# Regrouping the last weight loads and splitting the final accumulator of a decode block by output quadrants

## The chip, the cores and the metric

One core of one Trainium2 chip runs the whole program. The metric is the device time of one execution in microseconds (us). TensorE does the matmuls, VectorE (DVE) and ScalarE (ACT) the elementwise work, GpSimd (POOL) a few fills, and SyncE (SP) issues nearly all DMAs.

## The reference, cut to what matters

```python
h  = x + attention(layernorm(x), k_cache, v_cache, wq) @ wo      # x: 4 tokens x 448
y  = layernorm(layernorm(h))
g  = gelu(y @ w1 + b1)                                          # 4 x 1792
h2 = h + g @ w2 + b2                                            # 4 x 448
```

The case is a decode step: four tokens, one each, against a cache of 1024 positions in eight groups of heads. Nearly all of its bytes are the caches and the weights, read once. Only the last line, `h + g @ w2 + b2`, is touched here.

## The kernel before, in words

SP issues all loads in one fixed order: eleven packed streams with queries, keys, values and output weights, then the last values, the last output weights, `w1`, and `w2`. They go through a ring of three slots of SBUF, so a load is issued when its slot is free, long before its data are wanted. TensorE's order is written out by hand; the other engines follow by semaphores.

**The second product of the MLP.** `w2` has 1792 rows. They are held as 14 chunks (`w2t[c]`): chunks 0 to 11 and the chunks 12 and 13, each 128 rows by 448 columns. The 448 output columns are four groups of C = 112. Output group j is computed on partitions 32j to 32j+31, called quadrant j. So each chunk is four matmuls of 128x32 weights (the transposed activations `gT`) with 112 columns of `w2`, one for each quadrant (line 510). A result that is first set up with `h + b2` (line 489) stays in one PSUM tile `py` for all four quadrants, and all 14 chunks add to it.

**How w2 is loaded (lines 380 to 389).** SP issues five pieces in this order: chunks 0 to 7 (1792 KB), chunks 8 to 10 (672 KB), then `w2_low` as two DMAs of 28 KB, then chunks 11 and 12 (448 KB), last the columns of quadrants 0 to 2 of chunk 13 (168 KB). `w2_low` is quadrant 3 of chunk 13, folded: its 128 rows are laid on 64 partitions as two pieces side by side, in DRAM as eight blocks of four rows (with a row left out between blocks), and the other 64 partitions are filled with zeros by POOL (line 381). In that form it takes two matmuls (line 516) with weights from `gT_low`, which DVE fills (line 506).

**The order on TensorE (lines 508 to 516).** The loop goes over c = 0 to 13 and j = 0 to 3; the two `w2_low` matmuls come in chunks 9 and 10 behind j = 1. The waits for the loads stand in this order: chunk 0 waits for the first piece, chunk 8 for the second, the first `w2_low` matmul for both small pieces, chunk 11 for the fourth, chunk 13 for the last.

**The end (lines 517 to 520).** DVE copies `py` to `res` in SBUF. Two DMAs of 4 KB store its halves: ACT issues the one of quadrants 2 and 3, SP the one of quadrants 0 and 1. Both wait for the copy. The program ends when both have landed.

**ACT before that.** Its last work is the gelu (line 480), with an activation table loaded for it ahead of time.

Of the kernel before, what the change touches and what calls it, by code (L numbers as in the profile page):

```python
# [8 lines left out]
F32 = mybir.dt.float32  # L9
# [6 lines left out]
B, D = 4, 448  # L16
# [4 lines left out]
P = 128  # L21
H = P // 2
ND = 4
NKC = W // P
NFC = F // P
FQ = F // 4
Q = 32
GAP = Q // B
LIFT = Q - B
# [34 lines left out]
W1C = 3 * F + F // 2  # L64
C = D // 4
PAD = 3 * (P - C)
W2L = NFC * D - C
EPS = 1e-5
SCALE = DH ** -0.5

# [1 line left out]
def block_kernel(ctx: ExitStack, tc, first, streams, v7, wo67, w1, w2, w2_low, out):  # L72
    nc = tc.nc
    const = ctx.enter_context(tc.tile_pool(name="const", bufs=1))
    ring = ctx.enter_context(tc.tile_pool(name="ring", bufs=3))
    work = ctx.enter_context(tc.tile_pool(name="work", bufs=2))
    once = ctx.enter_context(tc.tile_pool(name="once", bufs=1))
    ps_s = ctx.enter_context(tc.tile_pool(name="ps_s", bufs=2, space=PSUM))
    ps_t = ctx.enter_context(tc.tile_pool(name="ps_t", bufs=1, space=PSUM))
    ps_o = ctx.enter_context(tc.tile_pool(name="ps_o", bufs=1, space=PSUM))  # L80
    ps_m = ctx.enter_context(tc.tile_pool(name="ps_m", bufs=2, space=PSUM))
    ps_w = ctx.enter_context(tc.tile_pool(name="ps_w", bufs=1, space=PSUM))
# [80 lines left out]
    pT = [const.tile([P, NKC // 2, B, Q], F32, name=f"pT{i}") for i in range(2)]  # L163
    oT = [const.tile([P, 4, Q], F32, name=f"oT{i}") for i in range(2)]
    gT = const.tile([P, NFC, LIFT + Q], F32, name="gT")
    gT_low = const.tile([P, 2, Q], F32, name="gT_low")
    idle = const.tile([P, 512], BF16, name="idle")
    nc.vector.memset(idle, 0.0)
    back = const.tile([P, 4, LIFT + Q], F32, name="back")
# [4 lines left out]
    def beside(t, j):  # L174
        return t[:, :Q] if j % 2 == 0 else t[:, LIFT:]
# [48 lines left out]
    def scores(g):  # L224
        s = [ps_s.tile([P, 512], F32, tag="s", name=f"s{g}_{h}") for h in range(2)]
        mx = work.tile([P, 2], F32, tag="mx", name=f"mx{g}")
        for h in range(2):
            for c in range(2):
                for b in range(B):
                    nc.tensor.matmul(  # L230
                        s[h][b * Q : (b + 1) * Q, :], qT[g % 2][:, c, b, :], load_k(g, h, c)[:, b, :],
                        start=(c == 0), stop=(c == 1),
                    )
            nc.vector.reduce_max(mx[:, h : h + 1], s[h], axis=AX.X)  # L234
        nm = work.tile([P, 1], F32, tag="nm", name=f"nm{g}")
        nc.vector.tensor_max(nm, mx[:, 0:1], mx[:, 1:2])
        nc.vector.tensor_scalar_mul(nm, nm, -SCALE)  # L237
        p = work.tile([P, 2 * 512], F32, tag="p", name=f"p{g}")
        sums = work.tile([P, 2], F32, tag="sums", name=f"sums{g}")
        for h in range(2):  # L240
            nc.scalar.activation(  # L241
                p[:, h * 512 : (h + 1) * 512], s[h], AF.Exp, bias=nm, scale=SCALE,
                accum_out=sums[:, h : h + 1],
            )
        rec = work.tile([P, 1], F32, tag="rec", name=f"rec{g}")
        nc.vector.tensor_add(rec, sums[:, 0:1], sums[:, 1:2])
        nc.vector.reciprocal(rec, rec)
        return p, rec
# [24 lines left out]
        return po  # L273


    acc = ps_w.tile([P, D], F32, name="acc")


    def columns(t, j):
# [4 lines left out]
    def heads(g, po, rec):  # L284
        o = work.tile([P, 2, DH], F32, tag="o", name=f"o{g}")
        nc.vector.tensor_scalar_mul(o[:, :, :P], po[:, :, :P], rec)  # L286
        nc.scalar.mul(o[:, :, P:], po[:, :, P:], rec)  # L287
        pt = ps_m.tile([P, 512], F32, tag="m", name=f"pot{g}")
        if g in (HKV - 3, HKV - 1):
            keep_warm(3 if g == HKV - 1 else 5, pt)  # L290
        for c in range(2):
            for i in range(2):
                at = (2 * i + c) * P - i * REP
                nc.tensor.transpose(pt[:, at : at + P], o[:, i, c * P : (c + 1) * P], ident)  # L294
        if g >= HKV - 2:
            keep_warm(1)
        dst = oT[g % 2].rearrange("p (r c) (b e) -> p r (c b) e", r=REP, b=B)[..., 0]
        src = pt.rearrange("p (i k q) -> p q k i", i=2, q=Q)[:, :REP]
        nc.vector.tensor_reduce(dst, src, axis=AX.X, op=ALU.add)
# [60 lines left out]
    for g in range(HKV):  # L360
        if g + 1 < HKV:
            p, rec_next = scores(g + 1)
            if g == HKV - 2:
                heads(g - 1, *late)
            if g + 2 < HKV:
                project_q(g + 2, wq_parts(part("q", g + 2)))
            transpose_p(g + 1, p)
            if g + 1 == HKV - 1:
                keep_warm(2, ps_m.tile([P, 512], F32, tag="m", name="wait"))
                tail.append(ps_t.tile([P, 2, 512], F32, tag="t", name="tail"))  # L370
                keep_warm(5)
        else:
            v7t = load_v7()
            tw = slot("w1")
            wo_last = [wo_rows(tw[:, i * WC : (i + 1) * WC]) for i in range(2)]
            nc.sync.dma_start(tw[:, : 2 * WC], wo67)
            tw1 = tw[:, 2 * WC : 2 * WC + W1C]
            for a, n in ((0, 2 * F), (2 * F, W1C - 2 * F)):
                nc.sync.dma_start(tw1[:, a : a + n], w1[:, a : a + n])
            tw2 = slot("w2")  # L380
            nc.gpsimd.memset(tw2[H:, W2L : W2L + 2 * C], 0.0)
            at = 0
            for n in (8 * D, 3 * D, 0, 2 * D, 3 * C):
                if n:
                    nc.sync.dma_start(tw2[:, at : at + n], w2[:, at : at + n])
                else:
                    for h in range(2):
                        nc.sync.dma_start(tw2[h * Q : (h + 1) * Q, W2L : W2L + 2 * C], w2_low[h, :, : Q // 8, :])
                at += n
        if g == HKV - 1:  # L390
            keep_warm(5)
        po = values(g, v7t if g == HKV - 1 else None)
        if g == HKV - 2:
            project_o(g - 1, wo_rows(part("o", g - 1)))
        if g == HKV - 3:
            late = po, rec
        else:
            heads(g, po, rec)
        if g < HKV - 3:
            project_o(g, wo_rows(part("o", g)))  # L400
        if g == HKV - 2:
            accs = once.tile([P, 4 * P], F32, tag="u", name="accs")[:, :D]
            nc.scalar.copy(accs, acc)
            hsum = ps_s.tile([P, 512], F32, tag="s", name="hsum")[:, :P]
            ph = hsum.rearrange("p (i c) -> p i c", i=2)
            pu = ps_s.tile([P, 512], F32, tag="s", name="pu")[:, :FQ]
            for j in range(4):
                nc.tensor.matmul(ph[j * Q : (j + 1) * Q], sel, columns(accs, j), start=True, stop=False)  # L408
        if g == HKV - 1:
            keep_warm(5)  # L410
            for i in range(2):
                project_o(HKV - 2 + i, wo_last[i])
        if g + 1 < HKV:
            rec = rec_next

    w1t = [tw1[:, a * F : (a + 1) * F] for a in range(3)] + [tw1[:, 3 * F :]]
    w2t = [tw2[:, c * D : (c + 1) * D] for c in range(NFC)]
# [17 lines left out]
    h = once.tile([P, P], F32, tag="h", name="h")  # L435
    hb = once.tile([P, PAD + P + C], F32, tag="hb", name="hb")
# [26 lines left out]
    for a in range(ND):  # L463
        for j in range(4):
            rows, w = w1_part(a, j)
# [14 lines left out]
        nc.scalar.activation(u[:, cols], u[:, cols], AF.Gelu_apprx_tanh)  # L480

    keep_warm(2)
    py = ps_o.tile([P, C], F32, tag="o", name="py")
    for i in range(2):
        for j in range(4):
            if i <= j:
                at = PAD + C * j - P * (j - 1 + i) if j else PAD
                lhs = back[:, j - 1 + i if j else 0, :]
                nc.tensor.matmul(
                    py[j * Q : (j + 1) * Q], beside(lhs, j), hb[:, at : at + C], start=(i == 0), stop=False,  # L490
                )
    keep_warm(2)
    res = once.tile([P, P], F32, tag="res", name="res")
    nc.gpsimd.memset(res, 0.0)
    put = ps_m.tile([P, 3 * P], F32, tag="m", name="put")
    for c in range(3):
        nc.tensor.transpose(put[:, c * P : (c + 1) * P], u[:, c * P : (c + 1) * P], ident)
# [5 lines left out]
    halves = put2.rearrange("p (s j i b e) -> p s i j b e", s=2, j=2, i=2, b=B)[..., 0]  # L503
    for side, i, rows in ((0, 0, slice(0, H)), (1, 1, slice(H, P))):
        nc.vector.tensor_copy(gT[rows, 12:NFC, LIFT:Q], halves[rows, side, i])
    nc.vector.tensor_copy(gT_low[:H, :, :B], halves[:H, 0, :, 1])
    nc.tensor.matmul(tail[0][:Q, 0, :Q], gT[:, 0, :Q], gT[:, 0, :Q], start=True, stop=True)
    for c in range(NFC):
        for j in range(4 if c < NFC - 1 else 3):
            nc.tensor.matmul(  # L510
                py[j * Q : (j + 1) * Q], beside(gT[:, c, :], j), w2t[c][:, j * C : (j + 1) * C],
                start=False, stop=(c == NFC - 1 or (c == NFC - 2 and j == 3)),
            )
            if j == 1 and 9 <= c < 11:
                w = tw2[:, W2L + (c - 9) * C : W2L + (c - 8) * C]
                nc.tensor.matmul(py[3 * Q :], gT_low[:, c - 9, :], w, start=False, stop=False)  # L516
    nc.vector.tensor_copy(res[:, :C], py)  # L517
    for i, queue in ((1, nc.scalar), (0, nc.sync)):
        at = i * H + LIFT
        queue.dma_start(out[2 * B * i : 2 * B * (i + 1)], res[at : at + 2 * B])  # L520


# [67 lines left out]
```

## Time and profile before

| | |
|---|---|
| median of 3 runs | 213.80 us (213.77 to 213.82) |
| the profiled execution's own time | 213.79 us |
| its span in the trace | 212.0 us |
| mean granted TensorE clock | 0.871 |
| DMA, mean over the span | 417 GB/s |

The profile is one execution. Times in its rows count from the start of the span; the execution's own time is 1.8 us longer than the span. PE is a matmul, PEld a weight load, SPq and ACTq are DMA issues of SP and ACT. In this trace each matmul of line 510 shows as two records of each kind.

### The profile page before, as it was taken

The numbers are of one execution on the slowest core, as the hardware profiler recorded it, in microseconds if no ns is written. First come the engines' busy times: TensorE is split into PE (matmuls) and PEld (weight loads), VectorE is DVE, ScalarE is ACT, GpSimd is POOL, SyncE is SP. The second block draws the span as 40 slices with busy tenths as digits, with TensorE's granted clock in tenths as the row PEclk, the third lists the DMA queues.
The fourth block names the chain that finished last, engine by engine and source line by source line (L and its number), as shares of the span: only waits on it lengthen the run. The fifth ranks groups of instructions, "written<-read, shape, count | busy, mean of one in ns | idle before, by whom it ended". The sixth has DMA issues, their size and how long they took to land.

```text
span 212.0 us, 2559 instructions
## 1 busy us (share of the span) xinstructions
PE 142.4 (67%) x1103; PEld 55.5 (26%) x1103; DVE 37.0 (17%) x153; ACT 24.5 (12%) x58; POOL 6.5 (3%) x22
## 2 busy tenths in 40 slices
PE   0469805861860885870794780586499998989994
PEld 0333301220110511220122120131124333335443
DVE  1521400320130110320123011031032032101330
ACT  2011300110001100210003000030002002100310
POOL 6200000000000000000000000000000000000110
PEclk9999975896697579996589698599589999999999
DMA  7999798999989999898999989899999899999991
GB/s 297 437 407 510 340 512 383 460 446 398 480 355 507 393 449 452 386 483 347 510 414 436 468 383 469 365 490 398 464 414 444 378 467 399 408 434 417 416 404 58
DMA packets 3146, 88.39 MB, mean 417 GB/s; under 512 B 368, under 2 KB 576, under 8 KB 960
## 3 DMA queue, kind: packets, MB, share of 16 engines
q1 hardware_dynamic: 3120, 88.24, 97.0%
q8 instruction: 8, 0.13, 0.2%
q14 instruction: 2, 0.02, 0.0%
q10 hardware_dynamic: 16, 0.00, 0.0%
HBM read 88.23 MB, written 0.01 MB: 416 GB/s over the span
## 4 chain that ended last, share of the span: by engine, by line
DMA 79%; PE 18%; ACT 1%; issue 0%; SPq 0%; DVE 0%; ACTq 0%
DMA stream<-stream 69%; DMA w<-w 10%; PE s L230 6%; PE po L269 6%; PE ppt L255 2%; PE py L510 2%; PE pq L207 1%; PE pqt L215 1%; ACT qs L209 1%; PE acc L304 0%; SPq L98 0%; SPq L100 0%; DVE res L517 0%; PE py L516 0%; ACTq L209 0%
## 5 line engine op out<-in xcount | busy, mean ns | idle before, releaser
L230 PE MATMUL s<-stream,qT 128*32 128x512 f32 x256 | 37.4, 730 | 17.1 <-DMA stream<-stream 17.1
L269 PE MATMUL po<-stream,pT 128*32 128x512 f32 x224 | 31.6, 702 | 17.5 <-DMA stream<-stream 17.5
L234 DVE TENSOR_REDUCE mx<-s 128x1 f32<-128x512 f32 x16 | 11.1, 691 | 57.3 <-PE s L230 57.3
L230 PEld LDWEIGHTS s<-stream,qT 128*32 128x32 f32 x256 | 9.7, 132 | 42.6 <-issue 30.6
L207 PE MATMUL pq<-stream,yT 128*32 128x512 f32 (+1 forms) x80 | 10.2, 603 | 9.7 <-DMA stream<-stream 6.6
L269 PEld LDWEIGHTS po<-stream,pT 128*32 128x32 f32 x224 | 6.9, 124 | 35.3 <-DMA stream<-stream 20.4
L286 DVE TENSOR_SCALAR o<-po,rec 128x256 f32<-128x256 f32 x8 | 3.9, 483 | 60.1 <-PE po L269 60.1
L209 ACT COPY qs<-pq 128x512 f32<-128x512 f32 x8 | 4.7, 585 | 83.3 <-PE pq L207 83.3
L287 ACT ACTIVATE o<-po,rec 128x256 f32<-128x256 f32 x8 | 3.8, 473 | 74.4 <-DVE o L286 74.4
L241 ACT ACTIVATE p<-s,nm 128x512 f32<-128x512 f32 x16 | 10.9, 689 | 10.1 <-DVE nm L237 10.1
L255 PE MATMUL ppt<-ident,p 128*128 128x128 f32 x64 | 11.1, 303 | 0.4
L304 PE MATMUL acc<-stream,oT 128*32 128x448 f32 x48 | 7.3, 683 | 5.2 <-DMA stream<-stream 4.0
L215 PE MATMUL pqt<-ident,qs 128*128 128x128 f32 x32 | 6.1, 322 | 5.7 <-ACT qs L209 5.7
L294 PE MATMUL pot<-ident,o 128*128 128x128 f32 x32 | 7.1, 317 | 3.8 <-DVE o L286 3.1
L354 PEld LDWEIGHTS <-idle 128*32 128x32 bf16 x70 | 6.3, 96 | 9.0 <-issue 3.6
L207 PEld LDWEIGHTS pq<-stream,yT 128*32 128x32 f32 x80 | 4.1, 124 | 17.1 <-issue 16.0
L255 PEld LDWEIGHTS ppt<-ident,p 128*128 128x128 f32 x64 | 7.6, 151 | 3.7 <-ACT p L241 3.7
L354 PE MATMUL tail<-idle 128*32 128x512 bf16 x28 | 7.6, 381 | 0.0
L294 PEld LDWEIGHTS pot<-ident,o 128*128 128x128 f32 x32 | 3.4, 148 | 13.3 <-DVE o L286 10.5
L354 PE MATMUL wait<-idle 128*32 128x512 bf16 x30 | 6.8, 380 | 0.0
L215 PEld LDWEIGHTS pqt<-ident,qs 128*128 128x128 f32 x32 | 3.9, 159 | 10.3 <-ACT qs L209 8.6
L462 POOL MEMSET u<- 128x64 f32 x1 | 0.2, 151 | 175.3 <-PE hsum L408 175.3
(128 smaller groups left out, 79.3 us busy)
## 6 DMA issues: line engine op xcount, KB each, us to landing
stream<-stream SPq DMA_DIRECT2D x5, 7040.0 KB, 35.8
stream<-stream SPq DMA_DIRECT2D x3, 6912.0 KB, 39.3
stream<-stream SPq DMA_DIRECT2D x2, 4992.0 KB, 16.1
stream<-stream SPq DMA_DIRECT2D x1, 7168.0 KB, 40.2
w<-w SPq DMA_DIRECT2D x2, 1792.0 KB, 21.4
v<-v SPq DMA_DIRECT2D x1, 3072.0 KB
w<-wo SPq DMA_DIRECT2D x1, 1792.0 KB, 19.6
w<-w SPq DMA_DIRECT2D x1, 1344.0 KB
```

What stands on the lines that cost most here:

```text
L207: nc.tensor.matmul(pq[j * Q : (j + 1) * Q, cols], yT[:, a, :], w, start=True, stop=True)
L209: nc.scalar.copy(qs, pq)
L215: nc.tensor.transpose(pt[:, i * P : (i + 1) * P], qs[:, i * P : (i + 1) * P], ident)
L230: nc.tensor.matmul(s[h][b * Q : (b + 1) * Q, :], qT[g % 2][:, c, b, :], load_k(g, h, c)[:, b, :], start=(c == 0), stop=(c == 1),)
L234: nc.vector.reduce_max(mx[:, h : h + 1], s[h], axis=AX.X)
L241: nc.scalar.activation(p[:, h * 512 : (h + 1) * 512], s[h], AF.Exp, bias=nm, scale=SCALE, accum_out=sums[:, h : h + 1],)
L255: nc.tensor.transpose(pt[:, c, :], p[:, c * P : (c + 1) * P], ident)
L269: nc.tensor.matmul(po[b * Q : (b + 1) * Q], pT[g % 2][:, c, b, :], vt[:, :, b, :], start=(c == 0), stop=(c == NKC // 2 - 1),)
L294: nc.tensor.transpose(pt[:, at : at + P], o[:, i, c * P : (c + 1) * P], ident)
L304: nc.tensor.matmul(acc[i * Q : (i + 1) * Q, :], oT[g % 2][:, i, :], wt[:, i, :], start=(g == 0), stop=(g == HKV - 3),)
L354: nc.tensor.matmul(to[:Q, :512], idle[:, :Q], idle, start=True, stop=True)
L510: nc.tensor.matmul(py[j * Q : (j + 1) * Q], beside(gT[:, c, :], j), w2t[c][:, j * C : (j + 1) * C], start=False, stop=(c == NFC - 1 or (c ...
```

## The change

Quadrant 2 of chunk 13 moves from the last load to `w2_low`, which then has 2 x 56 KB; quadrants 0 and 1 of chunk 11 move from the fourth load to the second. Five pieces stay: 1792, 784, 2 x 56, 336 and 112 KB. The accumulator becomes two tiles: `py0` for quadrants 0 and 1 in the place of `py`, `py1` for quadrants 2 and 3 in the place of `acc`, which is a sum of an earlier stage. TensorE's order changes: the `w2_low` matmuls, now four, come ahead of chunk 8, and chunk 12 ends quadrants 2 and 3. ACT copies quadrants 2 and 3 and issues their store; DVE copies quadrants 0 and 1, and SP issues their store.

```diff
-W2L = NFC * D - C
+W2L = NFC * D - 2 * C
...
-    gT_low = const.tile([P, 2, Q], F32, name="gT_low")
+    gT_low = const.tile([P, 2, LIFT + Q], F32, name="gT_low")
...
-    acc = ps_w.tile([P, D], F32, name="acc")
+    acc = ps_w.tile([P, D], F32, tag="w", name="acc")
...
-            nc.gpsimd.memset(tw2[H:, W2L : W2L + 2 * C], 0.0)
+            nc.gpsimd.memset(tw2[H:, W2L : W2L + 4 * C], 0.0)
             at = 0
-            for n in (8 * D, 3 * D, 0, 2 * D, 3 * C):
+            for n in (8 * D, 3 * D + 2 * C, 0, D + 2 * C, 2 * C):
                 if n:
                     nc.sync.dma_start(tw2[:, at : at + n], w2[:, at : at + n])
                 else:
                     for h in range(2):
-                        nc.sync.dma_start(tw2[h * Q : (h + 1) * Q, W2L : W2L + 2 * C], w2_low[h, :, : Q // 8, :])
+                        nc.sync.dma_start(tw2[h * Q : (h + 1) * Q, W2L : W2L + 4 * C], w2_low[h, :, : Q // 8, :])
...
-    py = ps_o.tile([P, C], F32, tag="o", name="py")
+    pys = [ps_o.tile([P, C], F32, tag="o", name="py0"), ps_w.tile([P, D], F32, tag="w", name="py1")[:, :C]]
+
+    def py(j):
+        return pys[j // 2][j * Q : (j + 1) * Q]
...
-    res = once.tile([P, P], F32, tag="res", name="res")
-    nc.gpsimd.memset(res, 0.0)
+    res = [once.tile([P, P], F32, tag=f"res{i}", name=f"res{i}") for i in range(2)]
+    for i in range(2):
+        nc.gpsimd.memset(res[i], 0.0)
...
-    nc.vector.tensor_copy(gT_low[:H, :, :B], halves[:H, 0, :, 1])
+    nc.vector.tensor_copy(gT_low[:H, :, LIFT:Q], halves[:H, 0, :, 1])
     nc.tensor.matmul(tail[0][:Q, 0, :Q], gT[:, 0, :Q], gT[:, 0, :Q], start=True, stop=True)
-    for c in range(NFC):
-        for j in range(4 if c < NFC - 1 else 3):
...
-            if j == 1 and 9 <= c < 11:
-                w = tw2[:, W2L + (c - 9) * C : W2L + (c - 8) * C]
-                nc.tensor.matmul(py[3 * Q :], gT_low[:, c - 9, :], w, start=False, stop=False)
-    nc.vector.tensor_copy(res[:, :C], py)
-    for i, queue in ((1, nc.scalar), (0, nc.sync)):
+
+    def second(c, j, stop=False):
+        nc.tensor.matmul(py(j), beside(gT[:, c, :], j), w2t[c][:, j * C : (j + 1) * C], start=False, stop=stop)
+
+    for c in range(8):
+        for j in range(4):
+            second(c, j)
+    for i in range(2):
+        for j in (2, 3):
+            at = W2L + (2 * i + j - 2) * C
+            nc.tensor.matmul(py(j), beside(gT_low[:, i, :], j), tw2[:, at : at + C], start=False, stop=False)
+    for c in range(8, 11):
+        for j in range(4):
+            second(c, j)
+    for c, j in ((11, 0), (11, 1), (11, 2), (11, 3), (12, 2), (12, 0), (12, 3), (12, 1), (13, 0), (13, 1)):
+        second(c, j, stop=c == (13 if j < 2 else 12))
+    nc.scalar.copy(res[1][H:, :C], pys[1][H:])
+    nc.vector.tensor_copy(res[0][:H, :C], pys[0][:H])
+    for i, queue in enumerate((nc.sync, nc.scalar)):
         at = i * H + LIFT
-        queue.dma_start(out[2 * B * i : 2 * B * (i + 1)], res[at : at + 2 * B])
+        queue.dma_start(out[2 * B * i : 2 * B * (i + 1)], res[i][at : at + 2 * B])
```

On the host, `w2_low` is built with 4C columns in place of 2C, and `w2` ends after 2C columns of chunk 13 in place of 3C.

## Rows read from the trace of the kernel before

**Rows 1.** The page: DMA over the span in 40 slices, then the longest shares of the chain
```profile
DMA  7999798999989999898999989899999899999991
DMA 79%; PE 18%; ACT 1%; issue 0%; SPq 0%; DVE 0%; ACTq 0%
```

**Rows 2.** The chain that ended last, in time: start us, us, what
```profile
184.30 21.43 DMA w<-w
205.73 0.04 issue
205.78 2.14 PE py L510 x74
```

**Rows 3.** Busy time by stretches: length, each engine, then PEclk, DMA share, GB/s
```profile
206.00:206.50 0.50, 0.50 (x32) 0.50 (x28) 0.00 (x0) 0.00 (x0) 0.00 (x0) 1.00 1.01 376
207.00:207.50 0.50, 0.50 (x28) 0.34 (x20) 0.00 (x0) 0.00 (x0) 0.00 (x0) 1.00 0.62 219
207.50:208.00 0.50, 0.50 (x26) 0.50 (x25) 0.00 (x0) 0.00 (x0) 0.00 (x0) 1.00 0.44 164
208.00:208.50 0.50, 0.50 (x16) 0.39 (x7) 0.00 (x0) 0.00 (x0) 0.00 (x0) 1.00 0.25 89
208.50:209.00 0.50, 0.50 (x21) 0.40 (x22) 0.00 (x0) 0.00 (x0) 0.00 (x0) 1.00 0.00 0
```

**Rows 4.** Timeline of weight loads of line 510, from three narrow windows
```profile
205.78 1.50 PEld L510 LDWEIGHTS py<-w,gT 128*32 128x32 f32 x64 [0.30 <-DMA w<-w]
207.43 0.24 PEld L510 LDWEIGHTS py<-w,gT 128*32 128x32 f32 x10 [0.16 <-DMA w<-w]
208.53 0.35 PEld L510 LDWEIGHTS py<-w,gT 128*32 128x32 f32 x16
208.95 0.15 PEld L510 LDWEIGHTS py<-w,gT 128*32 128x32 f32 x6
```

**Rows 5.** Loads of w2: issues in time, then size and us from issue to landing
```profile
184.67 0.43 SPq L385 DMA_DIRECT2D w<-w  x1
185.15 2.68 SPq L388 DMA_DIRECT2D w<-w_low  x2
189.62 0.34 SPq L385 DMA_DIRECT2D w<-w  x1
193.91 0.33 SPq L385 DMA_DIRECT2D w<-w  x1
...
w<-w SPq DMA_DIRECT2D x1, 672.0 KB, 22.7
w<-w SPq DMA_DIRECT2D x1, 448.0 KB, 18.9
w<-w SPq DMA_DIRECT2D x1, 168.0 KB, 15.0
```

**Rows 6.** Lines 516 and 510: duration ns min/median/max, first and last start us
```profile
L516 PEldq EVENT_SEMAPHORE  x2: 51/51/51, 207.5 to 207.6; - x2
L510 PE MATMUL py<-w,gT x110: 258/259/284, 205.8 to 209.1; 128*32 128x112 f32 x110
```

**Rows 7.** Timeline of the end: last matmuls, the copy, the two stores
```profile
208.28 1.06 PE L510 MATMUL py<-w,gT 128*32 128x112 f32 x24
209.40 0.27 DVE L517 COPY res<-py 128x112 f32<-128x112 f32 x1 [3.60 <-PE py L510]
209.74 0.32 SPq L520 DMA_DIRECT2D out<-res  x1
209.75 0.64 ACTq L520 DMA_DIRECT2D out<-res  x1
```

**Rows 8.** ACT, then POOL, by shapes: busy us, mean ns, idle before
```profile
L209 ACT COPY qs<-pq 128x512 f32<-128x512 f32 x8 | 4.7, 585 | 83.3 <-PE pq L207 83.3
L480 ACT ACT_TABLE_LOAD x1 | 1.3, 1283 | 0.0
L343 ACT COPY rs<-pb 128x448 f32<-128x448 f32 x1 | 0.5, 532 | 2.2 <-PE pb L342 2.2
L454 ACT ACTIVATE junk<-dh 128x128 f32<-128x128 f32 x1 | 0.3, 309 | 5.0 <-DVE dh L444 5.0
...
L494 POOL MEMSET res<- 128x128 f32 x1 | 0.2, 241 | 0.0
```

**Rows 9.** Timelines of ACT's gelu and POOL's fill of the w2 slot
```profile
203.96 0.69 ACT L480 ACTIVATE u<-u 128x256 f32<-128x256 f32 x2 [3.62 <-DVE u L479]
186.03 0.28 POOL L381 MEMSET w<- 64x224 f32 x1
```

More of the change, by code (lines that the diff above doesn't have):

```diff
@@ L489, in block_kernel @@
                 nc.tensor.matmul(
-                    py[j * Q : (j + 1) * Q], beside(lhs, j), hb[:, at : at + C], start=(i == 0), stop=False,
+                    py(j), beside(lhs, j), hb[:, at : at + C], start=(i == 0), stop=False,
                 )
     keep_warm(2)
-    res = once.tile([P, P], F32, tag="res", name="res")
-    nc.gpsimd.memset(res, 0.0)
+    res = [once.tile([P, P], F32, tag=f"res{i}", name=f"res{i}") for i in range(2)]
+    for i in range(2):
+        nc.gpsimd.memset(res[i], 0.0)
     put = ps_m.tile([P, 3 * P], F32, tag="m", name="put")
@@ L505, in block_kernel @@
         nc.vector.tensor_copy(gT[rows, 12:NFC, LIFT:Q], halves[rows, side, i])
-    nc.vector.tensor_copy(gT_low[:H, :, :B], halves[:H, 0, :, 1])
+    nc.vector.tensor_copy(gT_low[:H, :, LIFT:Q], halves[:H, 0, :, 1])
     nc.tensor.matmul(tail[0][:Q, 0, :Q], gT[:, 0, :Q], gT[:, 0, :Q], start=True, stop=True)
-    for c in range(NFC):
-        for j in range(4 if c < NFC - 1 else 3):
[L510 to L513, printed above, removed]
-            if j == 1 and 9 <= c < 11:
-                w = tw2[:, W2L + (c - 9) * C : W2L + (c - 8) * C]
-                nc.tensor.matmul(py[3 * Q :], gT_low[:, c - 9, :], w, start=False, stop=False)
-    nc.vector.tensor_copy(res[:, :C], py)
-    for i, queue in ((1, nc.scalar), (0, nc.sync)):
+    def second(c, j, stop=False):
[15 more added lines that the diff above has]
+    for i, queue in enumerate((nc.sync, nc.scalar)):
         at = i * H + LIFT
-        queue.dma_start(out[2 * B * i : 2 * B * (i + 1)], res[at : at + 2 * B])
+        queue.dma_start(out[2 * B * i : 2 * B * (i + 1)], res[i][at : at + 2 * B])
 def kernel(A_x, A_k_cache, A_v_cache, A_wq, A_wo, B_x, B_w1, B_b1, B_w2, B_b2):
@@ L569 @@
     ])
-    w2_low = np.zeros((2, 8, Q // 8 + 1, 2 * C), np.float32)
-    w2_low[:, :, : Q // 8] = w2[-1, :, 3 * C :].reshape(2, H, C).transpose(1, 0, 2).reshape(2, 8, Q // 8, 2 * C)
-    w2 = np.concatenate([w2[:-1].transpose(1, 0, 2).reshape(P, -1), w2[-1, :, : 3 * C]], axis=1)
+    w2_low = np.zeros((2, 8, Q // 8 + 1, 4 * C), np.float32)
+    w2_low[:, :, : Q // 8] = w2[-1, :, 2 * C :].reshape(2, H, 2 * C).transpose(1, 0, 2).reshape(2, 8, Q // 8, 4 * C)
+    w2 = np.concatenate([w2[:-1].transpose(1, 0, 2).reshape(P, -1), w2[-1, :, : 2 * C]], axis=1)
     arrays = {
```

## The prediction

> **What bounds the kernel now.** I read the page first: the DMA engines are at 0.9 or more in most slices and the chain that ended last is 79% DMA [rows 1]. Up to the end this is a kernel that waits for its bytes, and the change leaves every load ahead of `w2` alone. So only the last microseconds can move, and the chain in order of time says where they begin: one wait of 21.43 us for `w2` ends at 205.73, and from there TensorE works on the second product [rows 2].
>
> The stretches show what the loads do meanwhile. Up to 206.5 the 16 DMA engines are all busy (share 1.01); then the share falls to 0.62, 0.44 and 0.25, and to 0.00 by 208.5 [rows 3]. Some engines have finished while a few late ones still bring the rest, and a load has landed only with its last part. TensorE's granted clock is 1.00 in each of these stretches, its higher level (2.4 GHz), though TensorE waited between them, so the clock is no term here.
>
> The weight loads of line 510 then show four starts [rows 4]. Chunks 0 to 7 start at 205.78 behind the first piece. Chunk 8 starts at 207.43; the second piece was issued at 184.67 and landed 22.7 later, at 207.37 [rows 5]. Chunk 11 starts at 208.53, behind the fourth piece (189.62 + 18.9 = 208.52), and chunk 13 at 208.95, behind the last (193.91 + 15.0 = 208.91) [rows 4, 5]. The last matmul ends at 208.28 + 1.06 = 209.34, DVE copies from 209.40 to 209.67, the stores are issued at 209.74 and 209.75 [rows 7]. So each landing costs, and the last three steps are a fixed tail.
>
> **The rate of one quadrant.** 64 records took 1.50 us on four quadrants [rows 4], 16 to each: 0.094 us a record, and a matmul is two records. The last record needs 0.26 us to its end [rows 6].
>
> **Part 1: the loads.** No byte is added. The second piece landed 207.37 - 205.73 = 1.64 us behind the first, 672 KB, so 410 KB per us [rows 2, 5]. Its 112 KB more cost 0.27 us: it lands at 207.64.
>
> For `w2_low` no landing time is shown. In the kernel before, the two waits for it, at 207.5 and 207.6, took 51 ns each [rows 6], so it had landed by 207.5. Now it is behind 112 KB more, and has 56 KB more of its own: 0.14 us at the rate above, or 0.27 us if its eight blocks use half of the 16 engines. Upper bound: 207.5 + 0.27 + 0.27 = 208.04. Lower bound: it is no later than the second piece, 207.64. With about 0.05 us from a landing to the first weight load (207.37 to 207.43), TensorE starts again between 207.70 and 208.09. I take 207.95, nearer to the upper end, because `w2_low` stands behind the second piece in SP's queue and the late engines decide.
>
> The page "DMA: Bandwidth & Descriptors" of the Trainium skill, in its section on why a DMA increments its semaphore by 16, says that a DMA runs on the largest number of engines up to 16 that divides the slowest dimension of both sides; eight blocks would then be eight engines. That speaks against moving bytes into this load, and no row here shows the number of engines. By the rule the extra is 0.27 us, without it 0.14.
>
> The fourth piece has 56 KB more ahead of its end (1232 KB against 1176 behind the first piece): 208.52 + 0.14 = 208.66, between 208.52 and 208.79. The last has the same 1344 KB: 208.91, give or take 0.14.
>
> SP issues the same number of DMAs, over 14 us before they land [rows 5]. POOL's larger fill (0.28 us at 186.03) and second fill of `res` (0.24 us) have microseconds of cover until TensorE and the copies need them [rows 8, 9]. DVE's copy to `gT_low` has the same size. All of these I cost at nothing; uncovered they would cost their own length, 0.3 us at most.
>
> **Part 2: the order on TensorE.** This is where a wait is added. The `w2_low` matmuls now stand ahead of chunk 8, so chunks 8 to 11, whose data have landed or nearly so, queue behind `w2_low`'s landing. Before, TensorE restarted at 207.43; now at 207.95. What is left for quadrants 2 and 3 is two `w2_low` matmuls and chunks 8 to 12: seven matmuls, 14 records each. The last one begins at 207.95 + 13 x 0.094 = 209.17 and ends at 209.43. The fourth piece is wanted after ten records, at 208.89, and is there. Compared with 209.34, quadrants 2 and 3 end 0.09 later although they skip chunk 13.
>
> Quadrants 0 and 1 reach chunk 13 at 207.95 + 10 x 0.094 = 208.89, wait for the last piece until 208.95, and end at 208.95 + 0.09 + 0.26 = 209.30. DVE's copy and SP's issue follow at the old distances (0.06, 0.27, 0.07): store at 209.70, 0.04 earlier than before.
>
> **Part 3: ACT's copy and store.** ACT's copies from PSUM took 0.585 for 512 columns and 0.532 for 448 [rows 8]: 0.83 ns a column, so 112 columns give 0.585 - 400 x 0.00083 = 0.25 us. An ACT instruction of 128 columns took 0.31 [rows 8], which I keep as the upper end; DVE's copy of this shape took 0.27 [rows 7]. Start 209.49, end 209.74, and with the old 0.08 from copy to issue the store goes out at 209.82: 0.07 us later than before. ACT's issue took 0.64 beside SP's, which took 0.32 [rows 7]. Now 0.12 apart, it may take less, by 0 to 0.32; I take 0, since SP's store would then end last and has gained only 0.04.
>
> **Sum.** Quadrants 2 and 3 end 0.09 later, and ACT's copy is 0.02 shorter than DVE's: +0.07 on the profiled 213.79, which is 0.01 under the median of 213.80. Forecast 213.86 us. A measurement of this kernel can tell 0.2%, 0.43 us, from no change, so this is no change.
>
> **The rivals.**
>
> *The landing of w2_low is hidden.* TensorE starts at 207.70. Quadrants 2 and 3 end at 209.18, ACT's store goes out at 209.57, and SP's, at 209.70, is last: 213.75, or 213.61 if the last piece lands 0.14 earlier because the late engines carry less of it. For it: the 51 ns waits [rows 6]. Against: everything in `w2_low` now waits behind a longer second piece. About 213.7.
>
> *The landing of w2_low comes much later.* This is the case on the slow side. Each 0.1 us that TensorE starts later is 0.1 us at the end, since quadrants 2 and 3 have work without a gap. It passes 0.2% if the start is at 208.31 or later, so if the two changed pieces cost 0.9 us and not 0.54; a start at 208.45 gives 214.36. For it: the late engines (share 0.44 at 207.5 to 208 [rows 3]). Against: it needs more delay than the upper bound of bytes gives.
>
> *ACT loads another table for its copy.* 1.28 us [rows 8], which in the open gives 215.14. It decides only if the copy is not in the gelu's table and the load waits with the copy. ACT has nothing to do between 204.65 and 209.4 [rows 9], and eight copies ran among other activations with only one load shown for the gelu at line 480 [rows 8]. The page "ScalarE: Activation LUTs" of the Trainium skill, section on table sets, has copy among the functions that every set holds; the rows agree for the sets before the gelu.
>
> *The late engines are relieved.* If the new sizes evened out the lag, all pieces would land by about 208.4, 0.5 us earlier, and the end would move to some 213.3. Nothing in the rows says that the late engines are those that lose bytes.
>
> If ACT's copy waited for quadrants 0 and 1 as well, it would cost nothing (209.30 is ahead of 209.43).
>
> **How the numbers follow.** Chances: forecast 0.66, hidden landing 0.22, later landing 0.06, table 0.02, relief 0.04. The first two are within 0.2%: same 0.88, slower 0.08, faster 0.04. Bounds: a start at 208.09 (+0.14) with a copy of 0.31 (+0.06) gives 214.06; the second case goes down to 213.61. With 0.1 on either side for what ACT's issue may give and what the stores' landing may take: 213.50 to 214.15.
>
> **What would show it.** Right: the first weight loads of `w2_low` at about 207.95 with idle time ahead of them put down to a DMA; no wait at chunk 11; ACT's copy some 0.25 us long at 209.5. Wrong: a start at 207.7 or beyond 208.3, a gap ahead of chunk 11 or 12, a table load between the gelu and the copy, or ACT's store issued ahead of SP's.

## The result and the profile after

| | before | after |
|---|---|---|
| median | 213.78 us (22 runs, 213.68 to 213.93) | 214.09 us (22 runs, 213.79 to 214.26) |
| ratio | | 1.0014, 95% interval 1.0007 to 1.0020 |
| profiled execution, its span | 213.79, 212.0 us | 214.07, 212.3 us |

The change makes the kernel slower by 0.31 us, 0.14%. That is inside the 0.2% that the prediction counted as no change, but the interval of the ratio leaves out 1; the forecast was 213.86. In a second set of runs the changed kernel stood at 213.98 beside 213.77 (e7 below), so the loss is 0.2 to 0.3 us.

Where the time went is read first from the chain that ended last in the changed kernel (start us, us, what), the counterpart of [rows 2]:

```profile
187.20 20.66 DMA w<-w_low
207.86 0.14 issue
208.00 0.29 PE py L523 x2
...
209.65 0.27 DVE res L530
```

Before, the chain ran through the first piece of `w2`, and `w2_low` was nowhere in it as a wait. Now the landing of `w2_low` at 207.86 is the last wait in the chain. The timeline of the changed kernel from the first piece on (start us, us, instruction, idle time before it) answers to [rows 4, 7]:

```profile
205.87 1.50 PEld L515 LDWEIGHTS py<-w,gT 128*32 128x32 f32 x64 [0.31 <-DMA w<-w]
207.97 0.14 PEld L523 LDWEIGHTS py<-w,gT_low 128*32 128x32 f32 x3 [0.60 <-issue]
208.00 0.29 PE L523 MATMUL py<-w,gT_low 128*32 128x112 f32 x2 [0.39 <-DMA w<-w_low]
208.22 1.10 PEld L515 LDWEIGHTS py<-w,gT 128*32 128x32 f32 x40
208.34 1.22 PE L515 MATMUL py<-w,gT 128*32 128x112 f32 x38
209.62 0.25 ACT L529 COPY res<-py 64x112 f32<-64x112 f32 x1 [4.88 <-PE py L515]
209.65 0.27 DVE L530 COPY res<-py 64x112 f32<-64x112 f32 x1 [3.75 <-PE py L515]
209.90 0.57 ACTq L533 DMA_DIRECT2D out<-res  x1
209.98 0.32 SPq L533 DMA_DIRECT2D out<-res  x1
```

Chunks 0 to 7 take their 1.50 us as before. Then TensorE stands until 207.97, where it went on at 207.43 before. The weight loads behind that run in one piece of 1.10 us, so TensorE as a whole does not stand still again, and the last matmul ends at 208.34 + 1.22 = 209.56 against 209.34 [rows 7]. These 0.22 us and 0.05 us behind them (2.72 us from the last matmul to the end of the span against 2.67) make the 0.27 between the two spans. The standstill is seen in the stretches (length, busy time of each engine, PEclk, DMA share, GB/s), against [rows 3]:

```profile
207.50:208.00 0.50, 0.11 (x7) 0.04 (x2) 0.00 (x0) 0.00 (x0) 0.00 (x0) 1.00 0.48 181
208.00:208.50 0.50, 0.50 (x21) 0.50 (x25) 0.00 (x0) 0.00 (x0) 0.00 (x0) 1.00 0.33 111
208.50:209.00 0.50, 0.50 (x30) 0.50 (x24) 0.00 (x0) 0.00 (x0) 0.00 (x0) 1.00 0.00 0
```

TensorE is busy 0.11 of the 0.50 us from 207.5, where before it was busy throughout, while the late DMA engines (share 0.48) bring `w2_low` and what follows. The granted clock is 1.00 in all these stretches, before and after.

The views show no landing of `w2_low` in the kernel before. The traces keep a record of each landing; the last record of each load, in us from the start of the span, is:

| profile | first piece | second piece | w2_low | fourth piece | last piece |
|---|---|---|---|---|---|
| before | 205.73 | 207.39 | 207.37 | 208.48 | 208.91 |
| changed | 205.83 | 207.71 | 207.86 | 208.72 | 209.00 |
| e1 | 205.78 | 207.67 | 207.87 | 208.73 | 209.01 |
| e4 | 205.73 | 207.39 | 207.29 | 208.50 | 208.92 |
| e5 | 205.76 | 207.80 | 205.90 | 208.64 | 208.93 |
| e9 | 205.75 | 207.41 | 207.65 | 208.79 | 209.07 |

Before, `w2_low` landed beside the second piece; in the changed kernel it lands 0.15 behind it.

### The profile page after: what moved, and what is told of

The parts are those of the page before. It is cut to its first block, busy times and chain, and to the rows that moved or that the text cites. A ratio compares the mean times of both kernels' runs of the same rounds, so it can differ in the third digit from the quotient of the medians.

```text
span 212.3 us, 2566 instructions
## 1 busy us (share of the span) xinstructions
PE 145.2 (68%) x1105; PEld 56.6 (27%) x1105; DVE 37.1 (17%) x153; ACT 24.7 (12%) x59; POOL 7.0 (3%) x23
## 4 chain that ended last, share of the span: by engine, by line
DMA 80%; PE 16%; DVE 1%; SPq 1%; issue 1%; ACT 0%; ACTq 0%
DMA stream<-stream 59%; DMA v<-v 11%; DMA w<-w_low 10%; PE s L230 7%; PE po L269 3%; PE acc L304 2%; PE pot L294 1%; PE pq L207 1%; PE ppt L255 1%; PE py L515 1%; DVE o L286 0%; SPq L100 0%; PE pqt L215 0%; ACT qs L209 0%; PE py L523 0%
## 5 line engine op out<-in xcount | busy, mean ns | idle before, releaser
L230 PE MATMUL s<-stream,qT 128*32 128x512 f32 x256 | 40.0, 767 | 18.8 <-DMA stream<-stream 18.8
L230 PEld LDWEIGHTS s<-stream,qT 128*32 128x32 f32 x256 | 10.4, 140 | 46.5 <-issue 33.7
L207 PE MATMUL pq<-stream,yT 128*32 128x512 f32 (+1 forms) x80 | 10.9, 643 | 7.8 <-DMA stream<-stream 4.6
L304 PE MATMUL acc<-stream,oT 128*32 128x448 f32 x48 | 8.0, 750 | 4.5 <-DMA stream<-stream 3.3
```

The source lines that it names most:

```text
L207: nc.tensor.matmul(pq[j * Q : (j + 1) * Q, cols], yT[:, a, :], w, start=True, stop=True)
L230: nc.tensor.matmul(s[h][b * Q : (b + 1) * Q, :], qT[g % 2][:, c, b, :], load_k(g, h, c)[:, b, :], start=(c == 0), stop=(c == 1),)
L304: nc.tensor.matmul(acc[i * Q : (i + 1) * Q, :], oT[g % 2][:, i, :], wt[:, i, :], start=(g == 0), stop=(g == HKV - 3),)
```

## The experiments

Times are medians; the ratio is to the kernel before, run on the same chip, with its 95% interval. "Last matmul" is the end of the last matmul of the second product in each profile.

| run | median us | ratio (interval) | last matmul |
|---|---|---|---|
| before | 213.78 | | 209.34 |
| changed | 214.09 | 1.0014 (1.0007 to 1.0020) | 209.56 |
| e1 w2_low behind chunk 10 | 213.91 | 1.0006 (0.9998 to 1.0015) | 209.44 |
| e2 one accumulator | 213.93 | 1.0007 (0.9998 to 1.0016) | 209.61 |
| e3 split alone | 213.71 | 1.0001 (0.9992 to 1.0009) | 209.29 |
| e4 order alone | 213.79 | 0.9999 (0.9990 to 1.0008) | 209.35 |
| e5 w2_low loaded earlier | 213.86 | 1.0005 (0.9996 to 1.0014) | 209.35 |
| e6 last piece in four blocks | 214.49 | 1.0036 (1.0023 to 1.0048) | 209.98 |
| e7 changed again | 213.98 | 1.0010 (1.0002 to 1.0019) | 209.56 |
| e8 e5, stores exchanged | 213.84 | 1.0002 (0.9993 to 1.0011) | 209.31 |
| e9 second piece as before | 213.90 | 1.0005 (0.9996 to 1.0014) | 209.61 |
| e10 other order at the end | 214.11 | 1.0010 (1.0000 to 1.0019) | 209.57 |

**e1: the w2_low matmuls behind chunk 10.** From the changed kernel, in TensorE's order alone:

```diff
-    for i in range(2):
-        for j in (2, 3):
-            at = W2L + (2 * i + j - 2) * C
-            nc.tensor.matmul(py(j), beside(gT_low[:, i, :], j), tw2[:, at : at + C], start=False, stop=False)
     for c in range(8, 11):
         for j in range(4):
             second(c, j)
+    for i in range(2):
+        for j in (2, 3):
+            at = W2L + (2 * i + j - 2) * C
+            nc.tensor.matmul(py(j), beside(gT_low[:, i, :], j), tw2[:, at : at + C], start=False, stop=False)
```

> The changed kernel, with the four w2_low matmuls moved from ahead of chunk 8 to behind chunk 10; loads, banks, copies and stores stay. Theory A (the wait for w2_low, ahead of work that has its data, costs the time): TensorE starts chunk 8 at the landing of the second piece, about 207.80 in place of 207.97, quadrants 2 and 3 still have 14 records of 0.094, so everything behind is 0.15 to 0.2 us earlier: 213.92 us. Theory B (TensorE issues in order, and quadrants 0 and 1 and the two stores are held at the end): the end stays where it is, 214.05 to 214.10. Theory C (the loads ahead of w2 or the sizes of the pieces cost the time): 214.05 to 214.10 too, with the first piece of w2 landing at 205.8 and not 205.73.

Measured 213.91, beside theory A's 213.92. The weight loads in time, in this run's profile:

```profile
207.71 0.54 PEld L515 LDWEIGHTS py<-w,gT 128*32 128x32 f32 x24 [0.39 <-DMA w<-w]
208.23 0.21 PEld L526 LDWEIGHTS py<-w,gT_low 128*32 128x32 f32 x4
208.34 0.14 PEld L515 LDWEIGHTS py<-w,gT 128*32 128x32 f32 x4
208.43 0.21 PEld L526 LDWEIGHTS py<-w,gT_low 128*32 128x32 f32 x4
208.77 0.43 PEld L515 LDWEIGHTS py<-w,gT 128*32 128x32 f32 x16
```

Chunks 8 to 10 start at 207.71, behind the second piece, and `w2_low` runs without idle time behind them. The start is 0.26 earlier than in the changed kernel, the last matmul only 0.12: from 208.64 to 208.77 TensorE waits for the fourth piece, which landed at 208.73, ahead of what is left of chunk 11. So now the fourth and last pieces bound the end.

**e2: one accumulator.** The changed kernel's loads and order, with the old end:

```diff
-    pys = [ps_o.tile([P, C], F32, tag="o", name="py0"), ps_w.tile([P, D], F32, tag="w", name="py1")[:, :C]]
+    pys = ps_o.tile([P, C], F32, tag="o", name="py")
...
-    nc.scalar.copy(res[1][H:, :C], pys[1][H:])
-    nc.vector.tensor_copy(res[0][:H, :C], pys[0][:H])
-    for i, queue in enumerate((nc.sync, nc.scalar)):
+    nc.vector.tensor_copy(res[:, :C], pys)
+    for i, queue in ((1, nc.scalar), (0, nc.sync)):
...
```

> The changed kernel's loads and order of matmuls, with one accumulator, one copy by DVE and two stores behind it as before. Theory A (the wait for w2_low): the last matmul ends at 209.55 as in the changed kernel, the copy and the stores follow as before, and the time stays at 214.0 to 214.1. Theory B (the copy by ACT, or the stores issued one behind the other, cost the time): back to 213.8 to 213.9.

This run stays open. Its profile follows theory A: the last matmul ends at 209.61, as late as in the changed kernel, and that execution took 214.04. Its median of 213.93 lies between the two forecasts, and its runs spread from 213.69 to 214.11. From the last matmul to the end of the span it took 2.64 us, 0.08 less than the changed kernel. By the medians the split costs 0.16 beside the changed kernel's 214.09 and 0.05 beside e7's 213.98, both from other sets of runs, so it may cost nothing.

**e3: the split alone.** The kernel before with `py0`, `py1`, ACT's copy and store:

```diff
...
-    nc.vector.tensor_copy(res[:, :C], py)
-    for i, queue in ((1, nc.scalar), (0, nc.sync)):
+    nc.scalar.copy(res[1][H:, :C], pys[1][H:])
+    nc.vector.tensor_copy(res[0][:H, :C], pys[0][:H])
+    for i, queue in enumerate((nc.sync, nc.scalar)):
...
```

> The kernel before, its loads and its order of matmuls, with the accumulator in two tiles, ACT copying and storing quadrants 2 and 3, DVE and SP quadrants 0 and 1. Theory A (the wait for w2_low): no part of it is here, so 213.75 to 213.85. Theory B (ACT's copy and the order of the stores): ACT's store is issued first, SP's second and it lands some 0.1 later than alone, so 213.9 to 214.0.

Measured 213.71, 0.04 under theory A's range and well under theory B's; the interval holds no change, and of B's 213.9 to 214.0 (ratios of 1.0006 to 1.0010) it holds the lower part. Without the new loads the split shows no harm. (Here DVE's half comes first, as e10 takes up.)

**e4: the order alone.** The kernel before, with its two `w2_low` matmuls ahead of chunk 8; the new order at the end is not in it:

```diff
     for c in range(NFC):
+        for i in range(2 if c == 8 else 0):
+            w = tw2[:, W2L + i * C : W2L + (i + 1) * C]
+            nc.tensor.matmul(py[3 * Q :], gT_low[:, i, :], w, start=False, stop=False)
         for j in range(4 if c < NFC - 1 else 3):
...
-            if j == 1 and 9 <= c < 11:
```

> The kernel before, with its two w2_low matmuls moved ahead of chunk 8; loads, accumulator, copy and stores stay. In the kernel before w2_low landed with the second piece at about 207.4, so theory A expects no new wait of size: quadrant 3 has its 14 records either way, 213.75 to 213.9. If the order costs whatever the sizes of the pieces, 214.0 to 214.1.

Measured 213.79, and the weight loads show why:

```profile
207.40 0.14 PEld L511 LDWEIGHTS py<-w,gT_low 128*32 128x32 f32 x2
207.44 0.15 PEld L513 LDWEIGHTS py<-w,gT 128*32 128x32 f32 x6
```

With the old sizes `w2_low` landed at 207.29, TensorE begins it at 207.40 and chunk 8 starts 0.04 later, at its old time. So neither this order nor the split shows a cost by itself: the wait comes from the order together with the new sizes. The new sizes with the old order were not run; e1 and e5 come nearest.

**e5: w2_low loaded earlier.** From the changed kernel, in SP's order alone:

```diff
-            for n in (8 * D, 3 * D + 2 * C, 0, D + 2 * C, 2 * C):
+            for n in (8 * D, 0, 3 * D + 2 * C, D + 2 * C, 2 * C):
```

> The changed kernel, with SP issuing the two w2_low DMAs ahead of the second piece and not behind it; all else stays, TensorE's order too. Theory A (TensorE waits for w2_low ahead of chunk 8, after that the last landings bound it): the w2_low matmuls run at about 207.4, beside the end of chunk 7, with no wait of size; chunk 8 then starts when the second piece has landed, 207.8 to 207.95, quadrants 2 and 3 have 10 records and not 14 from there, and the end is set by the last piece (landing at about 209.0), as with w2_low behind chunk 10: last matmul ends at 209.40 to 209.45, 213.85 to 213.95 us. Theory B (TensorE's order at the end and the two stores cost the time): 214.05 to 214.10 as in the changed kernel.

Measured 213.86, in theory A's range. TensorE's order is that of the changed kernel, only the wait is gone:

```profile
207.28 0.40 PEld L523 LDWEIGHTS py<-w,gT_low 128*32 128x32 f32 x8
207.84 1.27 PEld L515 LDWEIGHTS py<-w,gT 128*32 128x32 f32 x44
```

The `w2_low` matmuls run at 207.28, right behind chunk 7, in time that was idle. The last matmul ends at 209.35, as in the kernel before, and 0.05 ahead of theory A's 209.40 to 209.45. In e1 and e5 two different edits take away the same wait, and both times the last matmul comes earlier, by 0.12 and 0.21.

**e6: the last piece in four blocks**, from e3. It tries to use the DMA engines that have finished early:

```diff
-                if n:
+                if n == 3 * C:
+                    nc.sync.dma_start(tw2[:, at : at + n], w2_last[:, : P // 4, :])
+                elif n:
...
```

> The split alone (two accumulators, ACT and DVE copy, loads and order of the kernel before), with the last piece, 168 KB, laid out in DRAM as four blocks of 32 rows with a row left out between, so that fewer DMA engines may carry it. Theory D (a few late DMA engines set every landing, others have been idle for up to 2 us by then): if the four blocks go to engines that finish early, the last piece lands at or before the fourth (208.45) and not at 208.9; the last matmul ends at about 209.2 and not 209.3, 213.6 us against 213.71 for the split alone. If they go to late engines, each carries 42 KB in place of 10.5 KB, at 26 KB per us 1.2 us more: 214.9 us.

Neither forecast came true in full. 214.49 (5 runs) is 0.8 slower than e3, on the side of late engines but short of the 214.9. In the chain the last piece is issued at 193.79 and lands at 209.54, where it landed at 208.91 before; from 208.0 on very few engines still move it:

```profile
193.79 15.75 DMA w<-w_last
```

```profile
208.00:208.50 0.50, 0.50 (x18) 0.44 (x9) 0.00 (x0) 0.00 (x0) 0.00 (x0) 1.00 0.15 48
208.50:209.00 0.50, 0.29 (x6) 0.11 (x8) 0.00 (x0) 0.00 (x0) 0.00 (x0) 1.00 0.10 35
```

A share of 0.15 and 0.10 of 16 engines is about two. The trace has four landing records for this load, at 208.39, 208.56, 209.18 and 209.54, where the 128-row load had sixteen. So fewer blocks do put a load on few engines, and two of these four are late. Which engines are late by habit was not found out.

**e7: the changed kernel once more**, unedited.

> The changed kernel once more, beside the others and with a second profile. Theory A: TensorE starts on w2_low 2.05 to 2.2 us behind the landing of the first piece, whatever that landing is, and the last matmul ends 1.6 us after that start; 214.05 to 214.10. Theory C (the loads ahead of w2 end later in the changed kernel): the first piece lands at 205.8 or later again, not at 205.73.

Its profile speaks against theory C. Its chain has the landing of `w2_low` at the same 207.86 (187.12 + 20.74), though its first piece came earlier:

```profile
205.78 1.50 PEld L515 LDWEIGHTS py<-w,gT 128*32 128x32 f32 x64 [0.29 <-DMA w<-w]
207.96 0.14 PEld L523 LDWEIGHTS py<-w,gT_low 128*32 128x32 f32 x3 [0.69 <-issue]
208.34 1.22 PE L515 MATMUL py<-w,gT 128*32 128x112 f32 x38
```

Chunk 0 starts at 205.78, as in the kernel before, and not at 205.87. The end is still 209.56, so what stands ahead of `w2` is not the cause. TensorE starts 2.22 us behind the landing of the first piece, 0.02 over theory A's range. The median, 213.98, is 0.07 under the forecast.

**e8: the stores exchanged**, on top of e5:

```diff
-    for i, queue in enumerate((nc.sync, nc.scalar)):
+    for i, queue in ((1, nc.sync), (0, nc.scalar)):
```

> w2_low loaded ahead of the second piece, as in the run before, and the two stores exchanged: SP stores the half that ACT copied, ACT the half that DVE copied, so that SP issues first. From the last matmul's end to the end of the span the runs so far took 2.69 to 2.74 us where ACT issued first and 2.63 to 2.67 where SP did. Theory E (the program's end waits longer when SP's store is the second): 2.63 to 2.66 us, 213.80 us. Rival (which engine stores what makes no difference): 2.70, 213.86 us.

SP did issue first, at 209.61, and ACT at 209.66, but the stretch from the last matmul to the end went from 2.70 only to 2.67, short of the 2.63 to 2.66 that were forecast. Which store goes first is worth some 0.03 us at most here; the theory is not shown. At 213.84 this is also the lowest median that the new loads gave, and it does not beat the kernel before.

**e9: the second piece as before.** From the changed kernel, with quadrants 0 and 1 of chunk 11 back in the fourth piece:

```diff
-            for n in (8 * D, 3 * D + 2 * C, 0, D + 2 * C, 2 * C):
+            for n in (8 * D, 3 * D, 0, 2 * D, 2 * C):
```

> The changed kernel, with quadrants 0 and 1 of chunk 11 back in the fourth piece: 672 KB and 448 KB in place of 784 and 336; w2_low keeps its 2 x 56 KB, TensorE's order stays. Theory A in two terms (0.27 us of w2_low's landing from the longer second piece, 0.27 from its own doubled size): w2_low lands 1.85 us behind the first piece and not 2.1, TensorE starts on it at about 207.7. The end is then set by the fourth piece (208.7) with chunks 11 to 13 of quadrants 0 and 1 behind it: last matmul at 209.45 to 209.55, 213.95 to 214.05 us. If the second piece's size does nothing, w2_low lands at 207.86 and the last matmul ends at 209.56, 214.05 us.

```profile
207.76 0.14 PEld L523 LDWEIGHTS py<-w,gT_low 128*32 128x32 f32 x3 [0.47 <-issue]
208.14 1.47 PE L515 MATMUL py<-w,gT 128*32 128x112 f32 x38
```

`w2_low` landed at 207.65 by this run's chain, and TensorE began it at 207.76, 0.2 earlier than in the changed kernel. So the longer second piece is worth about 0.2 us of `w2_low`'s landing, and the rest comes from its own size (theory A had 0.27 for either). The end did not gain: 209.61, since quadrants 0 and 1 have three chunks left behind the fourth piece. The time, 213.90, was 0.05 under theory A's range and 0.15 under the other forecast; it is the start at 207.76 that tells them apart.

**e10: another order at the end.** From the changed kernel:

```diff
-    ((11, 0), (11, 1), (11, 2), (11, 3), (12, 2), (12, 0), (12, 3), (12, 1), (13, 0), (13, 1))
+    ((11, 0), (11, 1), (12, 0), (12, 1), (11, 2), (11, 3), (12, 2), (12, 3), (13, 0), (13, 1))
```

> The changed kernel, with chunk 12 of quadrants 0 and 1 ahead of chunk 11 of quadrants 2 and 3 in TensorE's order; all else stays. In the changed kernel DVE's copy of quadrants 0 and 1 starts at 209.65 where the prediction had 209.36. Theory F (quadrants 0 and 1 are held because their chunk 12 stands behind matmuls of quadrants 2 and 3 that wait for their turn): DVE's copy starts at 209.5 to 209.55, ahead of ACT's, which stays at 209.62; SP's store then goes out first, and the span is some 0.05 shorter, 214.0 us. Rival (quadrants 0 and 1 are late from the start at 207.97 on): DVE's copy stays at 209.6 to 209.65, 214.05 us.

```profile
209.66 0.25 ACT L529 COPY res<-py 64x112 f32<-64x112 f32 x1 [4.98 <-PE py L515]
209.66 0.27 DVE L530 COPY res<-py 64x112 f32<-64x112 f32 x1 [3.84 <-PE py L515]
```

DVE's copy stays at 209.66 and the time at 214.11, near the rival's forecast, yet theory F was right about the hold. In the changed kernel, by the single records of its trace, quadrant 0 paused from the record at 208.73 to the one at 208.96, 0.23 in place of 0.096, and went on right behind quadrant 2's chunk 11. In e10 that pause is gone: the last record of quadrant 1 began at 209.20 and ended at 209.46, where it ended at 209.56 in the changed kernel (an end is here a record's start and its 0.26 us). What theory F had wrong is what follows from it. Both copies wait on one running count of TensorE's finished work, ACT's for a value that includes the last matmul of quadrant 3, DVE's for that of quadrant 1, which stands later in the order. In e10 quadrant 3 ended at 209.57, the count rose at 209.58 and 209.64, and DVE's copy followed the second rise, 0.20 after its own quadrants were done. So here the earlier end was counted only behind the one that stands before it in the order.

In e3 the order is the other way round, since quadrant 2's chunk 13 comes last, and DVE's copy goes first:

```profile
209.34 0.27 DVE L523 COPY res<-py 64x112 f32<-64x112 f32 x1 [3.56 <-PE py L515]
209.44 0.25 ACT L522 COPY res<-py 64x112 f32<-64x112 f32 x1 [4.81 <-PE py L515]
```

No run gave DVE a count of its own.

## Why the prediction was right, and what was off

**The forecast, no change, held**, with the median at 0.14% and inside the range; the size was off, +0.07 forecast and +0.31 measured. Part of that is margin: the bounds on the start and on ACT's copy alone gave 214.06 at most, and the median of 214.09 is inside only by the 0.1 that was added for the stores. In the profile the last matmul ended 0.13 later than the sum had it (209.56 for 209.43), and the way from there to the end took 0.07 longer (2.72 for 2.65).

**Right: the cause and the place.** The wait for `w2_low` ahead of chunk 8 was forecast to end at 207.95 and ended at 207.97 and 207.96 in two profiles (208.00 and 208.01 in e10 and e2, with the same loads and the same order there). e1 and e5 remove it in two ways; their medians are 0.18 and 0.23 under the first measurement of the changed kernel. In the one set that holds both, e5 is 0.12 under e7, and their runs overlap, so the profiles carry more of the proof than the times. e4 shows that the order without the sizes has no such wait. There was no wait for a load at chunk 11 or 12, as forecast.

The rule of the Trainium skill that was weighed there, page "DMA: Bandwidth & Descriptors", section on why a DMA increments its semaphore by 16, makes eight blocks eight engines; by it the prediction's estimate for doubled `w2_low` was 0.27 us, against 0.14 us if all engines share it. The trace agrees with the rule: each `w2_low` load has eight landing records, the other pieces of `w2` have sixteen. e4 and e9 have the same second piece, of 672 KB, and differ in the size of `w2_low`, which landed at 207.29 in the one and at 207.65 in the other, with the first piece within 0.02 us of each other. That is 0.36 us, or 0.28 against the kernel before (207.37), so nearer to 0.27 than to 0.14.

**Right: ACT's copy.** 0.25 us forecast, and no table load ahead of it; the rival of another table is out, in the activations by shape:

```profile
L480 ACT ACT_TABLE_LOAD x1 | 1.3, 1283 | 0.0
...
L529 ACT COPY res<-py 64x112 f32<-64x112 f32 x1 | 0.2, 248 | 4.9 <-PE py L515 4.9
```

**Off: "The last one begins at 207.95 + 13 x 0.094".** Quadrants 2 and 3 were to end at 209.43; by the single records quadrant 3 ended at 209.53. Both kept pace, quadrant 2 with a record every 0.096 from 208.00 to 209.24. The 0.10 is made of small terms that the sum left out: the start 0.02 later, 0.03 from the first weight load to the first matmul, 0.03 for quadrant 3's first record, and 0.02 from thirteen steps of 0.096 and not 0.094.

**Off: "Quadrants 0 and 1 reach chunk 13 at 207.95 + 10 x 0.094 = 208.89" and "DVE's copy and SP's issue follow at the old distances (0.06, 0.27, 0.07): store at 209.70".** These are the steps that failed outright. Quadrants 0 and 1 were to end at 209.30 and be stored first. They were held for 0.13 us at chunk 12 by the order and ended at 209.56, after quadrants 2 and 3; DVE's copy began at 209.65 and SP issued at 209.98, after ACT at 209.90. ACT's store ahead of SP's is one of the signs that the prediction itself named for being wrong. The step also took the copy as free to start when its own quadrants are done, and e10 shows that an earlier end of them moves nothing. So the end had no early half: both copies ran side by side at the later time, and the way from the last matmul to the end grew by 0.05 where the sum had it shrink by 0.02.

**The rivals.** A hidden landing is excluded by the idle time ahead of `w2_low` (0.60 us for the weight loads, which their row puts down to issue, and 0.39 for the matmuls, put down to the DMA), a much later one by the start at 207.97. Relief of the late engines was to bring all pieces in by about 208.4; the last two landed at 208.72 and 209.00, later than before. What e1 and e5 leave over the kernel before, 0.1 us, is not told apart from zero by their intervals. It would fit these later fourth and last pieces; that share of the loss stays open.

No version ran measurably faster than the kernel before. e3, at 213.71, has the lowest median, with an interval that holds no change.

## What to carry to other kernels

A load that was free because it landed beside another one can turn into a wait when bytes are put in front of it or into it, so check each wait's order against the new order of landings, not only the total of bytes. Where the order of an engine is written by hand, put what may land late behind work whose data are there (e1), or issue its load earlier (e5). Splitting a result into halves can pay only if a half is released by itself: look at what each copy's wait counts, and where the half's last matmul stands in the order (e10). That an early half makes this kernel faster is not shown; e3 had one, and its interval holds no change.

## What was not expected of the hardware

ACT's 4 KB store took 0.57 us to issue where it went first and 0.64 where it went 0.01 behind SP's [rows 7], so standing beside SP's issue explains little of its length; SP's took 0.32 in both. A load of 168 KB laid out in four blocks landed at 209.54, 0.6 us later than the same bytes over 128 rows in the kernel before. And TensorE did not start its matmuls strictly in the order of the program: in the changed kernel chunk 8 of quadrants 0 and 1 (line 515) began at 208.03, ahead of the second pair of `w2_low` matmuls (line 523), which stand before it but belong to quadrants that were still busy.

```profile
208.03 0.29 PE L515 MATMUL py<-w,gT 128*32 128x112 f32 x2
...
208.19 0.29 PE L523 MATMUL py<-w,gT_low 128*32 128x112 f32 x2
```
